# Values of a chunk in one row on TensorE: both halves of the heads behind both masks, in a kernel of linear attention and two expert layers

## The chip, the cores and the metric

One core of one Trainium2 chip. The metric is device time in microseconds (us), as a median of runs. "PE" is TensorE's matmuls, "PEld" its weight loads, DVE is VectorE, ACT is ScalarE, POOL is GpSimd, SP is SyncE, which here issues most DMAs.

## What is computed

The reference has three parts, one behind the other. The first is a linear attention with a complex decay for every channel, 4 batches of 8 heads, 768 steps, 48 channels per head:

```
for t in range(768):
    S = a[t] * S + outer(k[t], v[t])      # a complex, normalised to |a| <= 0.999
    y[t] = q[t] @ real(S)                 # per batch and head, S is 48 x 48
x = y as (3072 tokens, 384)
h = x @ w_in                              # 384 -> 2048
x = (h * tanh(softplus(h))) @ w_out       # 2048 -> 384
e = argmax(x @ w_gate + modality_bias)    # 8 experts, the best one per token
out = gate * relu(x @ w1[e]) @ w2[e]      # 384 -> 1024 -> 384
```

## The kernel before, in words

**Tiling.** The attention is cut into 24 chunks of 128 steps (six per batch, all eight heads at once), and two chunks form a unit. There are 12 units. A unit of 256 tokens then goes through the first dense layer in eight steps (`moe1_h`, `moe1_act`, `moe1_o`): on TensorE a half of such a step is nine matmuls into `ph` or six into `po`, about a microsecond of work. Such a half, or a few small matmuls, is what stands between the pieces of the attention on TensorE. The expert layer follows from about 655 us on.

**A chunk of attention.** `att_scores` (lines 541 to 584) makes for each group of four heads (`hg` 0 and 1):
- scores: four products of keys and queries into the PSUM tile `ps`, of which there is one buffer (lines 550 to 555);
- mask: one VectorE multiplication of `ps` with the causal mask into the SBUF tile `sc` (lines 557 to 559);
- values: for each head `v` times `sc`, and for all but the first chunk of a batch the old state `s0` times the queries added to it, into the PSUM tile `py` (lines 561 to 568). Even heads write partitions 0 to 63 of `py`, odd heads 64 to 127, so each of these matmuls uses 64 of TensorE's 128 columns. In the trace every product of this float32 kind is two matmuls.

At the end ScalarE copies `py` to `Y` (line 580), and two DMAs of SP's queue write it to `xT`, from which the dense layer reads. `sc` of both groups and `Y` share one tag with two buffers (`tag="sc"`, `bufs=2` of the pool `apw`), so the three tiles of a chunk go round in two places: the mask of group 1 of a chunk takes the place that `Y` of the chunk before had.

In these texts S0 and S1 are the scores of the two groups, M0 and M1 their masks, V0 and V1 their values.

**What sets the order.** Nothing is issued directly. Each piece of work is a "strand" of operations with a due time, and `Plan.run` (lines 165 to 247) simulates the engines by a table of costs (`Queue.cost`, lines 264 to 282) and writes out one fixed order for each engine. An operation is ready when the one before it in its strand has its planned result. `part()` (lines 118 to 123) turns several operations of one engine into a single one, between which nothing else is put. The table charges 0.11 us for a product whose output has 64 partitions, and nothing for going from one kind of matmul to another.

`state` of the next chunk (`att_state`) and its `scores` wait for the mark `y` of the chunk, which stands behind V1. `s0`, which V0 and V1 read, is the state that the strand of the chunk before has made (the wait for `s`, lines 573 and 574).

The lines of the profile are all L261 (the place in `Queue` where every operation is issued), so the groups are told apart by the names of their tiles.

Of the kernel before, what the change touches and what calls it, by code (L numbers as in the profile page):

```python
# [540 lines left out]
def att_scores(g, ins, ci, xT):  # L541
    nc, p = g.nc, g.plan
    u, c = divmod(ci, 2)
    cc = ci % 6
    QK, v, s0 = g.QK[u], g.vt[ci % 2], g.st[ci % 2]
    p.wait(f"QK{u}_0")
    py = g.aps.tile([128, 4, 128], F32, tag="py", name=f"py{ci}")
    sc = {}

    def scores(hg):  # L550
        ps = g.aps.tile([128, 4, 128], F32, tag="ps", name=f"ps{ci}_{hg}")
        with p.part():
            for h in range(4):
                nc.tensor.matmul(ps[:, h, :], QK[hg][0:96, h, 1, c, 0:128], QK[hg][0:96, h, 0, c, 0:128], start=True, stop=True)
        return ps

    def mask(hg, ps):
        sc[hg] = g.apw.tile([128, 4, 128], F32, tag="sc", name=f"sc{ci}_{hg}")
        nc.vector.tensor_mul(sc[hg], ps, g.mask.to_broadcast([128, 4, 128]))

    def values(hg):
        with p.part():
            for h in range(4):
                hh = hg * 4 + h
                o = py[(hh % 2) * 64:(hh % 2) * 64 + 64, hh // 2, :]
                nc.tensor.matmul(o, v[:, hh, :], sc[hg][:, h, :], start=True, stop=cc == 0)
                if cc > 0:
                    nc.tensor.matmul(o, s0[:, hh, :], QK[hg][0:96, h, 0, c, 0:128], start=False, stop=True)

    mask(0, scores(0))  # L570
    p.wait(f"QK{u}_1", f"v{ci}")
    ps = scores(1)
    if cc > 0:
        p.wait(f"s{ci - 1}")
    values(0)
    mask(1, ps)
    values(1)
    p.mark(f"y{ci}")
    Y = g.apw.tile([128, 4, 128], F32, tag="sc", name=f"Y{ci}")
    nc.scalar.copy(out=Y, in_=py)  # L580
    dst = xT.rearrange("(p a e) t -> a e p t", a=2, e=48)
    for a in range(2):
        with p.behind(f"x{u}"):
            nc.sync.dma_start(out=dst[a, :, :, ci * 128:(ci + 1) * 128], in_=Y[a * 64:a * 64 + 48])


def attention(g, ins, units, xT):
    p = g.plan
    for u in units:
        with p.strand(f"lanes {u}", {0: 5, 1: 45, 2: 100}.get(u, due(u) - 75)):  # L590
            if u:
                p.wait(f"D{u - 1}")
            if u > 2:
                p.wait(f"h{u - 3}")
            att_lanes(g, ins, u)
        with p.strand(f"ends {u}", {0: 8, 1: 55, 2: 110}.get(u, due(u) - 62)):
            p.wait(f"D{u}")
            att_ends(g, u)
        att_repack(g, u)
        if u + 1 < NU:  # L600
            att_load(g, ins, u + 1)
        for c in range(2):
            ci = 2 * u + c
            with p.strand(f"load v {ci}", due(u) - 50 if u else -17.5):
                if ci > 1:
                    p.wait(f"y{ci - 2}", f"s{ci - 2}")
                with p.behind(f"v{ci}"):
                    g.nc.sync.dma_start(out=g.vt[ci % 2][:, :, 0:48], in_=ins["v"][ci])
            with p.strand(f"state {ci}", due(u) - 45 + 6 * c):
                if ci:  # L610
                    p.wait(f"s{ci - 1}")
                att_state(g, ins, ci)
            with p.strand(f"scores {ci}", due(u) - 43 + 6 * c):
                if ci:
                    p.wait(f"y{ci - 1}")
                att_scores(g, ins, ci, xT)
# [1191 lines left out]
```

## Time and profile before

| | |
|---|---|
| median of 3 runs | 955.14 us (952.89 to 955.41) |
| the profiled execution, its own time | 951.5 us |
| its span in the profile | 949.6 us |
| PE busy | 874.9 us (92%), 6401 matmuls |
| PEld busy | 828.8 us (87%) |
| DVE busy | 732.7 us (77%) |
| ACT busy | 668.8 us (70%) |
| POOL busy | 175.2 us (18%) |
| mean granted clock of TensorE | 0.974 of full speed |

A busy share is a mean over stages with different limits: until about 70 us, when the attention has its first scores, TensorE is mostly idle, and the attention's last values are at 621 us. Matmuls overlap each other, and the end of one is modelled, so what a piece costs TensorE is best read from start to start: from its first row in the timeline to the first row of the piece behind it.

### The profile page before, as it was taken

To read this page: it belongs to the slowest core of one execution; us is meant where nothing else is said; L and a number is where in the kernel's file an instruction comes from. 1 tells how busy PE (TensorE), PEld (TensorE's weight loads), DVE (VectorE), ACT (ScalarE), POOL (GpSimd) and SP (SyncE) were. 2 spreads that over 40 slices of the span, in tenths; PEclk is the share of its full clock that TensorE was granted. 3 is DMA by queue.
4 is the path that set the end of the run, shared out by engine and by line. 5 is a ranking of instruction groups with operands and counts; after the bars stand their busy time and mean duration, and the time that the engine had idled before them with its cause. 6 is when DMAs were issued, how large, how long until landed. Compare 5 with 4: busy or idle time off the path is not lost.

```text
span 949.6 us, 17369 instructions
## 1 busy us (share of the span) xinstructions
PE 874.9 (92%) x6401; PEld 828.8 (87%) x6401; DVE 732.7 (77%) x1517; ACT 668.8 (70%) x1093; POOL 175.2 (18%) x237
## 2 busy tenths in 40 slices
PE   1489899999999999998999999999899999999993
PEld 1267789999999989998999999999799999999883
DVE  4989788889898988798889899764699865565541
ACT  5786969787968787887788787767754556556551
POOL 1021202112120221030303020202112034332211
PEclk9979899999999999999999999999799999999997
DMA  9923323425252534233524142305654767666730
GB/s 306 347 68 89 96 71 113 112 78 124 78 124 67 135 93 109 68 95 107 134 68 123 46 102 67 93 26 194 225 190 136 247 216 237 218 223 212 235 123 7
DMA packets 102749, 128.22 MB, mean 135 GB/s; under 512 B 34601, under 2 KB 76599, under 8 KB 102656
## 3 DMA queue, kind: packets, MB, share of 16 engines
q1 hardware_dynamic: 89680, 89.00, 31.4%
q0 software_dynamic: 12976, 38.03, 13.3%
q8 instruction: 52, 0.85, 0.4%
q14 instruction: 41, 0.34, 0.1%
HBM read 93.74 MB, written 14.82 MB: 114 GB/s over the span
## 4 chain that ended last, share of the span: by engine, by line
PE 46%; ACT 22%; issue 11%; DMA 9%; DVE 8%; POOL 2%; SPq 0%; ACTq 0%; POOLq 0%; DVEq 0%
PE ph L261 11%; PE po L261 10%; ACT u L261 9%; PE py L261 5%; PE ps L261 5%; DMA out<-oss,tt 5%; PE qhs L261 4%; ACT X L261 3%; ACT S L261 3%; PE pst L261 3%; PE qos L261 3%; PE pl L261 2%; DVE ar L261 1%; ACT gh L261 1%; ACT v L261 1%
## 5 line engine op out<-in xcount | busy, mean ns | idle before, releaser
L261 ACT ACTIVATE u<-u 128x512 f32<-128x512 f32 x384 | 237.8, 629 | 6.5
L261 PE MATMUL po<-wt,gh 128*128 128x392 f32 x768 | 206.7, 350 | 2.3 <-ACT gh L261 2.0
L261 PE MATMUL ph<-xh,wt 128*128 128x256 f32 x1152 | 193.5, 288 | 6.6 <-ACT xh L261 4.1
L261 PEld LDWEIGHTS ph<-xh,wt 128*128 128x128 f32 x1152 | 163.5, 191 | 11.5 <-ACT xh L261 4.8
L261 PEld LDWEIGHTS po<-wt,gh 128*128 128x128 f32 x768 | 135.2, 190 | 6.6 <-issue 2.9
L261 PE MATMUL po<-wt,gl 128*128 128x392 f32 x384 | 132.0, 344 | 2.1 <-DVE gl L261 2.1
L261 PE MATMUL qos<-v,hhs 128*128 128x384 f32 x432 | 111.8, 339 | 0.0
L261 POOL DMA_DIRECT2D QK<-X x120 | 65.6, 554 | 230.7 <-ACT xs L261 72.1
L261 PE MATMUL qhs<-y,v 128*128 128x256 f32 x792 | 103.1, 283 | 0.0
L261 PE MATMUL ph<-xl,wt 128*128 128x256 f32 x576 | 101.5, 285 | 1.6 <-DVE xl L261 1.4
L261 PEld LDWEIGHTS qhs<-y,v 128*128 128x128 f32 x792 | 98.7, 189 | 0.0
L261 DVE TENSOR_TENSOR v<-r1s,v 128x1536 fp32r<-128x1536 f32 x30 | 52.7, 1757 | 49.0 <-ACT v L261 46.1
L261 ACT ACTIVATE u<-ph 128x512 f32<-128x512 f32 x96 | 56.7, 591 | 45.6 <-PE ph L261 41.9
L261 DVE SCALAR_TENSOR_TENSOR u<-u,ph 128x512 f32<-128x512 f32 x96 | 65.5, 683 | 26.3 <-ACT u L261 26.1
L261 PEld LDWEIGHTS ph<-xl,wt 128*128 128x128 f32 x576 | 82.7, 191 | 3.2 <-DVE xl L261 3.1
L261 DVE TENSOR_TENSOR gl<-u,gh 128x512 fp32r<-128x512 f32 x96 | 65.7, 686 | 14.6 <-ACT gh L261 14.5
L261 ACT ACTIVATE gh<-u 128x512 fp32r<-128x512 f32 x96 | 60.1, 627 | 23.7 <-DVE u L261 23.6
L261 PEld LDWEIGHTS po<-wt,gl 128*128 128x128 f32 x384 | 72.9, 190 | 3.5 <-DVE gl L261 3.3
L261 PEld LDWEIGHTS qos<-v,hhs 128*128 128x128 f32 x432 | 75.3, 188 | 0.1
L261 POOL DMA_INDIRECT xg<-x,tt x27 | 42.3, 1568 | 167.5 <-PE pt L261 116.6
L261 PE MATMUL qos<-v,hls 128*128 128x384 f32 x216 | 72.6, 336 | 0.0
L261 ACT ACTIVATE hhs<-qhs 128x512 fp32r<-128x512 f32 x48 | 28.7, 599 | 59.2 <-PE qhs L261 58.2
(149 smaller groups left out, 1598.3 us busy)
## 6 DMA issues: line engine op xcount, KB each, us to landing
r0s<-in_w SPq DMA_DIRECT2D x30, 768.0 KB, 4.5
r1s<-in_w SPq DMA_DIRECT2D x30, 768.0 KB, 4.8
QK<-X POOLq DMA_DIRECT2D x72, 96.8 KB, 3.4
QK<-X SPq DMA_DIRECT2D x72, 96.8 KB, 3.7
r<-in_wo SPq DMA_DIRECT2D x8, 768.0 KB, 7.9
r<-in_wi SPq DMA_DIRECT2D x8, 768.0 KB, 13.5
X<-in_q POOLq DMA_DIRECT2D x12, 384.0 KB, 4.9
A<-in_ai POOLq DMA_DIRECT2D x12, 384.0 KB, 4.5
```

Source lines behind the costliest of these rows:

```text
L261: self.plan.add(self.name, *cost[:2], lambda: real(*a, **k), *cost[2:])
```

## The change

S1 no longer has V0 right behind it: M1 is planned straight after S1, and V0 and V1 together become one operation of the plan, which waits for both masks (and for the old state). No instruction is added or taken away, and no tile changes.

```
     def values(hg):
-        with p.part():
-            for h in range(4):
-                hh = hg * 4 + h
-                o = py[(hh % 2) * 64:(hh % 2) * 64 + 64, hh // 2, :]
-                nc.tensor.matmul(o, v[:, hh, :], sc[hg][:, h, :], start=True, stop=cc == 0)
-                if cc > 0:
-                    nc.tensor.matmul(o, s0[:, hh, :], QK[hg][0:96, h, 0, c, 0:128], start=False, stop=True)
+        for h in range(4):
+            hh = hg * 4 + h
+            o = py[(hh % 2) * 64:(hh % 2) * 64 + 64, hh // 2, :]
+            nc.tensor.matmul(o, v[:, hh, :], sc[hg][:, h, :], start=True, stop=cc == 0)
+            if cc > 0:
+                nc.tensor.matmul(o, s0[:, hh, :], QK[hg][0:96, h, 0, c, 0:128], start=False, stop=True)
 
     mask(0, scores(0))
     p.wait(f"QK{u}_1", f"v{ci}")
-    ps = scores(1)
+    mask(1, scores(1))
     if cc > 0:
         p.wait(f"s{ci - 1}")
-    values(0)
-    mask(1, ps)
-    values(1)
+    with p.part():
+        values(0)
+        values(1)
     p.mark(f"y{ci}")
```

## Rows read from the trace of the kernel before

**Rows 1.** Busy time by stretch: stretch and length, PE, PEld, DVE, ACT, POOL, clock, DMA.

```profile
150.00:250.00 100.00, 99.08 (x770) 95.23 (x770) 87.77 (x189) 82.39 (x144) 16.48 (x28) 1.00 0.36 99
250.00:350.00 100.00, 96.58 (x764) 92.56 (x763) 88.67 (x188) 81.13 (x145) 16.50 (x28) 1.00 0.36 96
...
625.00:700.00 75.00, 69.81 (x466) 67.74 (x466) 46.47 (x93) 53.94 (x82) 10.41 (x6) 0.93 0.49 167
```

**Rows 2.** Waits of PE and PEld: who for whom, us in total, times, longest.

```profile
PE ph L261 <- ACT xh L261: 4.1, 2, 2.7
PE pst L261 <- ACT KT L261: 2.7, 4, 0.8
...
PEld py L261 <- issue: 0.9, 4, 0.3
```

**Rows 3.** Instructions of the tile py: count, shortest, median and longest in ns.

```profile
L261 ACT COPY Y<-py x24: 567/587/598, 74.0 to 621.4; 128x512 f32<-128x512 f32 x24
```

**Rows 4.** Timeline of PE, one chunk: start, length of the run of rows, what.

```profile
269.01 1.05 PE L261 MATMUL ps<-QK 96*128 96x128 f32 x8
269.82 0.60 PE L261 MATMUL po<-wt,gh 128*128 128x392 f32 x2
...
270.97 0.51 PE L261 MATMUL ph<-xh,wt 128*128 128x256 f32 x3
...
272.04 1.05 PE L261 MATMUL ps<-QK 96*128 96x128 f32 x8
273.02 0.45 PE L261 MATMUL py<-sc,vt 128*64 128x128 f32 x4
273.29 0.40 PE L261 MATMUL py<-QK,st 96*64 96x128 f32 x4
273.51 0.44 PE L261 MATMUL py<-sc,vt 128*64 128x128 f32 x4
273.73 0.44 PE L261 MATMUL py<-QK,st 96*64 96x128 f32 x4
274.10 0.63 PE L261 MATMUL ph<-xh,wt 128*128 128x256 f32 x3
...
275.37 0.45 PE L261 MATMUL py<-sc,vt 128*64 128x128 f32 x4
```

**Rows 5.** Timeline of PE, first chunk of a batch (no old state).

```profile
224.65 1.06 PE L261 MATMUL ps<-QK 96*128 96x128 f32 x8
225.63 0.66 PE L261 MATMUL py<-sc,vt 128*64 128x128 f32 x8
226.22 0.55 PE L261 MATMUL pkt<-ident,X 128*128 128x128 f32 x3
```

**Rows 6.** Timeline of PE, a chunk whose S1 is followed by other work.

```profile
569.09 1.48 PE L261 MATMUL pst<-vt,KT 128*96 128x48 f32 x16
570.50 0.45 PE L261 MATMUL py<-sc,vt 128*64 128x128 f32 x4
```

**Rows 7.** Timeline of PE from 96 us, where weights are still being prepared.

```profile
96.46 0.94 PE L261 MATMUL pl<-r,ident 128*128 128x384 f32 x2 [1.79 <-ACT wt L261]
```

**Rows 8.** Timeline of DVE: an M0, the M1 of rows 4, and a later M1.

```profile
183.20 0.69 DVE L261 TENSOR_TENSOR sc<-ps,mask 128x512 f32<-128x512 f32 x1 [0.53 <-PE ps L261]
...
273.81 0.68 DVE L261 TENSOR_TENSOR sc<-ps,mask 128x512 f32<-128x512 f32 x1
...
430.88 0.69 DVE L261 TENSOR_TENSOR sc<-ps,mask 128x512 f32<-128x512 f32 x1 [0.31 <-DMA xT<-Y]
```

**Rows 9.** Timeline of PE: the S1 behind the first mask of rows 8, and that ahead of the last.

```profile
184.07 1.06 PE L261 MATMUL ps<-QK 96*128 96x128 f32 x8
...
428.34 1.12 PE L261 MATMUL ps<-QK 96*128 96x128 f32 x8
```

**Rows 10.** Instructions of the tile Y: its DMAs, from issue to landing.

```profile
DMA to landing us min/median/max: 1.9/2.6/4.7
```

**Rows 11.** Timeline of PE at the end of the first dense layer.

```profile
673.62 0.45 PE L261 MATMUL po<-wt,gl 128*128 128x392 f32 x1 [1.25 <-DVE gl L261]
```

## The prediction, made before the run

> **What bounds the kernel now.** I read the busy time by stretch first: between 150 and 350 us TensorE's matmuls cover 97 to 99% of the time, at a granted clock of 1.00 (2.4 GHz), with VectorE at 88% and ScalarE at 82% [rows 1]. The second view, the waits of TensorE, says what the rest is: a few gaps, such as those ahead of `pst` and `ph`, 2.7 and 4.1 us in all. Ahead of the values there is next to nothing, 0.9 us of issue in four pieces; TensorE never waits there for a mask [rows 2]. So from about 107 to 657 us TensorE sets the pace, and what shortens its sequence should shorten the kernel. The third view, TensorE's timeline around one chunk, tells what that sequence costs, read from start to start [rows 4].
>
> S0, with dense-layer matmuls behind it, takes 269.82 - 269.01 = 0.81 us. S1, of the same eight matmuls but with values behind it, takes 273.02 - 272.04 = 0.98. A values piece takes 274.10 - 273.02 = 1.08: its four blocks start 0.27, 0.22 and 0.22 us apart, and from the fourth to the next kind of work it is 0.37. A dense half inside a dense stretch takes 272.04 - 270.97 = 1.07, behind scores 270.97 - 269.82 = 1.15, and between V0 and V1 275.37 - 274.10 = 1.27. So entering the 64-column kind costs about 0.10 to 0.17 us plus 0.05 in its first block, and leaving it about 0.15 plus 0.10 in what follows. These costs are paid twice per chunk today. There are 24 chunks [rows 3], and in the timeline each has other work between V0 and V1; 22 have V0 right behind S1.
>
> **The change, part by part.** It removes no instruction and no DMA, and moves none past SP's or POOL's queue; M1 moves forward in VectorE's order, V0 backward in TensorE's.
>
> *One entry and one exit fewer.* Before, from S1 to the end of V1: 0.98 + 1.08 + 1.27 + 1.08 = 4.41 us. After, S1 is followed by the dense half: 0.81; that half stands behind scores and ahead of values: 1.07 + 0.08 + 0.10 = 1.25; the joined values are eight blocks: 0.27 + 6 x 0.22 + 0.37 = 1.96. Sum 4.02, a saving of 0.39 us. In the four first chunks of a batch a values piece is eight matmuls, 226.22 - 225.63 = 0.59 us, and S1 takes 0.98 there too [rows 5]: I take 0.17 for S1, 0.10 to 0.15 for the joined piece, 0.30 in all. In the two chunks where `pst` stands between S1 and V0 it takes 1.41 us [rows 6]; there S1's 0.17 is not paid, and the saving is 0.20 for the values and 0.10 for the entry, 0.30. Sum: 18 x 0.39 + 4 x 0.30 + 2 x 0.30 = 8.8 us.
>
> What of it lies on the path: the first two chunks run before 82 us, and at 96 us TensorE waits 1.79 us for ScalarE's work on weights [rows 7], which the change doesn't speed up. I count their 0.7 us as lost: 8.1. Bounds from rows: none of the switching cost comes back (0) if it is only put elsewhere, and at most 24 x 0.44 = 10.6 if V0's first block also loses its 0.05.
>
> The Trainium skill, "TensorEngine Tiling (Array Packing)", section Key Properties, says that changing the tiling mode drains TensorE. "TensorE: Matmul & The Clock Gate", section Single matmul latency, puts the drain of a matmul at some 0.17 us. An estimate from these two pages is 2 x 0.17 = 0.34 us per chunk, 7.5 for the 22 chunks that count. The rows give 8.1 for these, and I keep the rows.
>
> *The new wait: V0 behind M1.* Now M1 has all of V0 and the half behind it, 2.35 us, to finish. After, it has the one half (1.25 us) that the plan puts there, or two. In rows 4 S1's last matmul ends at 272.04 + 1.05 = 273.09. If M1 followed at once it would end 0.68 later [rows 8], at 273.8, while the half ends at 272.04 + 0.81 + 1.25 = 274.10: no stall, 0.3 us to spare. The nearest case in the trace is S1 itself, which must wait until M0 has freed `ps`: M0 ends at 183.89 [rows 8] and S1 starts at 184.07 [rows 9], with one half between S0 and S1 and no idle time. Behind a waiting values row stands all of TensorE's work, and behind `y` the copy `Y`, the DMAs to `xT` and the next state; they all come earlier or later together with V1's end, which by the sum comes 0.39 us earlier. I cost the wait itself at nothing; its ends are a gain of 0 and a loss of 1.1 us per chunk (the second rival).
>
> *M1 and the place of Y.* M1 of the second chunk of a unit writes where `Y` of the first stood. Once M1 already waited for that DMA, 0.31 us [rows 8]; the DMAs land after 1.9 to 4.7 us [rows 10]. There S1 ends at 428.34 + 1.12 = 429.46, M1 can't start before 430.88, and with one half between, TensorE would come to V0 at about 430.4 and wait until 431.6. I take one such stall of 1.1 us; bounds 0 and 12 of them, 13 us.
>
> **Sum.** 8.1 - 1.1 = 7.0 us. The profiled execution took 951.5 us, so one like it would take 944.5; the median stands 3.6 us above it, and 955.1 - 7.0 = 948.1 us is the forecast. Behind 657 us everything is taken to shift as a whole, since route, gathers and weight loads are started by work that comes after the attention.
>
> **Rivals.** *Part is given back.* The plan is one long simulation, and M1's new place shifts every later choice. Gaps such as those ahead of `pst` (2.7 us) and `ph` (4.1 us) [rows 2] could double; and at the end of the dense layer TensorE waits for VectorE's and ScalarE's work, 1.25 us before one matmul [rows 11], so part of the gain may be lost to waits there. For: TensorE is at 69.8 of 75 us in that stretch [rows 1]. Against: these gaps hang on copies that don't move. Price: 2 to 5 us off the gain, 950 to 953 us.
>
> *TensorE waits for M1.* The table of costs knows neither the place of `Y` nor how late VectorE really is. If the plan leaves one half between S1 and V0 and M1 comes as late as now, then in rows 4 it ends at 274.49, 0.4 after the 274.10 at which the half ends, and the stall eats the saving. In the chunk at 428 us M1 ends at 431.57 against 430.4: 1.1 lost. Halfway, 0.75 - 0.39 = 0.36 us lost in each of 22 chunks: 8 us slower, 963. It decides from the point where M1 starts more than 0.7 us behind S1's last matmul. For: VectorE is 88% busy, and M1 today starts 0.72 and 1.42 us behind it in these two chunks. Against: today's M1 is planned behind V0, so some 0.9 us of that is the plan's own choice, and the plan puts values in only when their masks are due; it can put in a second half.
>
> "TensorE: Matmul & The Clock Gate" of the Trainium skill, section The mechanism (Part 3), says that matmuls start and end strictly in program order and only weight loads are pulled ahead. By it the dense work behind a waiting V0 could not step in, as this rival has it; TensorE's idle time ahead of `pst` in the trace agrees [rows 2].
>
> *The change does not join what it says*: the plan might still put work between the values. Against: a `part()` is one operation, so I give it nothing.
>
> **How the numbers follow.** Main case 0.70: 943.5 to 951.5, the predicted time 948.1. Given back 0.18: 950 to 953. Waits for M1 0.12: about 963. About 0.3% (2.9 us, so 952.2 us) is what a measurement of this kernel can tell from no change. The main case lies wholly below that, and 0.10 of the second: faster 0.80. The rest of the second, 0.08, is the same; the third is slower, 0.12. The range goes from 943.5 (no stall for `Y`, no loss ahead of 107 us, and the 0.05) to 953, which leaves out the third case and the edges.
>
> **What would show it.** Right: one run of `py` rows of 32 matmuls per chunk (16 in four of them) of about 1.96 us, S1 at 0.81, M1 directly behind S1 on VectorE, no new wait of `py` for `sc`, and the attention's last values about 7 to 8 us earlier than 621. Wrong: `py` waiting for VectorE's `sc`, by more than 0.39 us per chunk; values still at 0.22 us per block but a first and last block that grew; or last values earlier by 8 us with the end of the kernel where it was.

## The result and the profile after

| | before | after |
|---|---|---|
| median of the runs made side by side | 954.62 us (952.89 to 955.41, 4 runs) | 943.51 us (941.0 to 945.95, 4 runs) |
| ratio, 95% interval | | 0.9886 [0.9855, 0.9917] |
| the profiled execution, its own time | 951.5 us | 941.0 us |
| mean granted clock of TensorE | 0.974 | 0.979 |

The kernel is faster by 11.1 us; by the interval of the ratio, by 7.9 to 13.8 us. The direction was forecast. The size was not: 7.0 us were forecast, and the new median lies at the very edge of the range.

The profile's first part after the change, span and busy time of each engine:

```profile
span 939.2 us, 17356 instructions
PE 862.4 (92%) x6401; PEld 824.3 (88%) x6401; DVE 732.4 (78%) x1517; ACT 667.8 (71%) x1093; POOL 173.3 (18%) x237
```

There are as many matmuls as before, and TensorE is busy 12.5 us less. VectorE and ScalarE do the same work in the same time. So the gain is in what the matmuls cost where they stand, and, as is shown below, in a few us of TensorE's clock.

Busy time by stretch after the change, the stretches of [rows 1]:

```profile
150.00:250.00 100.00, 98.06 (x775) 94.99 (x775) 87.26 (x185) 82.88 (x148) 16.45 (x28) 1.00 0.35 96
250.00:350.00 100.00, 95.79 (x766) 92.63 (x766) 87.49 (x188) 80.75 (x143) 16.47 (x28) 1.00 0.36 96
```

From 150 to 250 us there are 775 matmuls in place of 770, in less busy time. From 250 to 350 us there are 766 for 764, and 4.2 us without a matmul in place of 3.4: a part of what they saved is now spent waiting.

TensorE's timeline after the change, the chunk of [rows 4], from its S1 to the end of its values (lines left out are marked with dots):

```profile
267.49 1.05 PE L261 MATMUL ps<-QK 96*128 96x128 f32 x8
268.30 0.59 PE L261 MATMUL ph<-xh,wt 128*128 128x256 f32 x3
...
269.44 0.49 PE L261 MATMUL pkt<-ident,X 128*128 128x128 f32 x3
269.87 0.45 PE L261 MATMUL py<-sc,vt 128*64 128x128 f32 x4
...
271.46 0.44 PE L261 MATMUL py<-QK,st 96*64 96x128 f32 x4
271.83 0.55 PE L261 MATMUL pkt<-ident,X 128*128 128x128 f32 x3
```

S1 takes 268.30 - 267.49 = 0.81 us, as forecast, and the eight blocks of values stand in one row of 271.83 - 269.87 = 1.96 us, as forecast. The joined rows of the chunks from 122 us on, first chunks of a batch aside, all have this length but one. That one is the tenth chunk, at 278.69 us, where the place of `Y` matters. Timeline of VectorE there, its M1:

```profile
280.42 0.69 DVE L261 TENSOR_TENSOR sc<-ps,mask 128x512 f32<-128x512 f32 x1 [3.22 <-DMA xT<-Y]
```

and of TensorE, S1 and the values of the same chunk:

```profile
275.50 1.12 PE L261 MATMUL ps<-QK 96*128 96x128 f32 x8
...
278.69 0.45 PE L261 MATMUL py<-sc,vt 128*64 128x128 f32 x4
...
279.40 0.44 PE L261 MATMUL py<-QK,st 96*64 96x128 f32 x4
281.17 0.45 PE L261 MATMUL py<-sc,vt 128*64 128x128 f32 x4 [1.32 <-DVE sc L261]
```

Two things are to be seen. VectorE sat idle 3.22 us until the DMA of the earlier `Y` had left its place, and TensorE waited 1.32 us for the mask. And the wait stands in the middle of the row: V0 ran at 278.69, 1.7 us before its chunk's M1 began, and only V1 waited. The plan treats the joined values as one operation that waits for both masks; on the chip V0 waits for M0 alone.

The tile `Y` after the change, who waited for it (us, times), and its DMAs:

```profile
  DVE sc L261: 10.2, 8
...
DMA to landing us min/median/max: 1.9/2.7/6.6
```

So M1 now waits for the place eight times, 10.2 us in all, where before one 0.31 us was found [rows 8]. Seven of the eight end before TensorE comes to V1.

The waits of TensorE after the change (who for whom, us in total, times, longest):

```profile
PE ph L261 <- DVE xl L261: 5.3, 11, 1.3
...
PE pkt L261 <- ACT KT L261: 3.8, 8, 0.6
PE ph L261 <- ACT xh L261: 2.4, 5, 0.6
```

and two of these kinds in the kernel before:

```profile
PE pkt L261 <- ACT KT L261: 2.1, 4, 0.6
...
PE ph L261 <- DVE xl L261: 1.4, 5, 0.5
```

So the wait of `ph` for `xh` is smaller than in [rows 2], and small waits for `xl` and `KT` have grown.

**Where the time went, by stretch.** I took anchors that stand in both traces and compared their starts, and between them summed every piece of TensorE from its first row to the first row of the next piece, idle time apart.

- Before the first S0: 66.29 us before, 64.24 after, 2.05 us. No engine's order differs up to there. The clock does, as the next fence shows.
- First S0 to the first `ph` of the second unit (four chunks): 88.32 to 86.13, 2.2 us. A part of it is the clock, see below.
- From there to the first product of the expert layer (20 chunks): 528.54 to 522.55, 6.0 us. Pieces without waits (`pkt` holds the turned keys, `pst` what the next state is made of): values -3.54, scores -2.93, `po` -0.99, `pst` -0.52, `pkt` and `ph` together +0.48, `pr` -0.15, in all -7.6, of which some 1.7 are the clock, see below. Waits: `py` +1.32, `pkt` +1.74, `ph` +0.73, `pst` -1.65, `po` -0.57, in all +1.6.
- The expert layer: 251.8 against 252.0 us. It moves as a whole.

Busy time by stretch ahead of the attention, the kernel before:

```profile
50.00:60.00 10.00, 7.59 (x35) 4.95 (x34) 9.90 (x13) 9.97 (x18) 5.36 (x10) 0.67 0.35 93
60.00:70.00 10.00, 10.00 (x50) 8.27 (x50) 6.90 (x9) 7.96 (x14) 0.10 (x1) 0.65 0.29 68
```

and the kernel after:

```profile
50.00:60.00 10.00, 7.54 (x44) 5.27 (x43) 9.73 (x12) 9.97 (x18) 5.46 (x10) 0.83 0.39 100
60.00:70.00 10.00, 10.00 (x57) 7.57 (x58) 9.11 (x13) 7.93 (x15) 0.00 (x0) 0.83 0.22 61
```

The column behind POOL is the granted clock: 0.65 to 0.67 in one profiled execution, 0.83 in the other, in a stretch in which both do the same. The kernels of the experiments fall on both sides (0.67 and 0.72 for the first below, 0.80 and 0.83 for the second, whose order is the same up to there). So these 2 us belong to the execution and not to the change. Without them the pair of profiles differs by 10.4 - 2.05 = 8.4 us.

The clock differs in two later places too. After TensorE's waits at 96 us [rows 7] it is 0.50 (1.2 GHz) for a while, before:

```profile
97.64:104.46 6.82, 4.65 (x16) 3.63 (x17) 6.02 (x10) 6.82 (x12) 0.00 (x0) 0.50 0.01 2
```

and after:

```profile
101.24:104.65 3.41, 3.41 (x18) 3.39 (x18) 3.30 (x5) 3.41 (x8) 0.00 (x0) 0.50 0.00 0
```

Three matmuls into `ph` take 1.01 us at the low clock where they take 0.51 at the high one (rows below and [rows 4]), so half of the busy time there is lost, 2.3 against 1.7 us. The first S0 of the kernel before, still in the slow stretch, costs 0.3 us more than the other's. By this estimate 0.9 of the 2.2 us ahead of the second unit are the clock. The other place is the longest wait for `xh` in the kernel before, TensorE's timeline:

```profile
442.26 0.92 PE L261 MATMUL ph<-xh,wt 128*128 128x256 f32 x3 [2.75 <-ACT xh L261]
443.39 1.01 PE L261 MATMUL ph<-xl,wt 128*128 128x256 f32 x3 [0.22 <-DVE xl L261]
...
445.98 0.87 PE L261 MATMUL ph<-xh,wt 128*128 128x256 f32 x6
...
448.12 0.52 PE L261 MATMUL ph<-xh,wt 128*128 128x256 f32 x3
```

and the windows of the same stretch:

```profile
442.30:445.80 3.50, 3.28 (x14) 2.99 (x15) 2.48 (x4) 3.47 (x5) 0.00 (x0) 0.51 0.22 90
```

Up to 445.98 fifteen matmuls take 3.50 us, the wait of 0.22 taken off; the next eighteen take 2.14, so fifteen would take 1.8. That is a loss of some 1.7 us. The changed kernel has no wait of this length there and none of the loss: its clock is 1.00 from 150 to 650 us.

### The profile page after: what moved, and what is told of

The parts are those of the page before. It is cut to its first block, busy times and chain, and to the rows that moved or that the text cites. A ratio compares the mean times of both kernels' runs of the same rounds, so it can differ in the third digit from the quotient of the medians.

```text
span 939.2 us, 17356 instructions
## 1 busy us (share of the span) xinstructions
PE 862.4 (92%) x6401; PEld 824.3 (88%) x6401; DVE 732.4 (78%) x1517; ACT 667.8 (71%) x1093; POOL 173.3 (18%) x237
## 4 chain that ended last, share of the span: by engine, by line
PE 33%; ACT 26%; DVE 14%; issue 12%; DMA 10%; POOL 2%; SPq 0%; ACTq 0%; POOLq 0%; DVEq 0%
ACT u L261 11%; PE ph L261 8%; PE po L261 7%; DMA out<-oss,tt 5%; ACT S L261 4%; PE qhs L261 4%; ACT X L261 3%; DMA xT<-Y 3%; PE qos L261 3%; PE ps L261 3%; PE py L261 3%; DVE S L261 3%; ACT gh L261 2%; DVE ar L261 2%; PE pst L261 2%
## 5 line engine op out<-in xcount | busy, mean ns | idle before, releaser
L261 PEld LDWEIGHTS ph<-xh,wt 128*128 128x128 f32 x1152 | 162.6, 190 | 10.4 <-ACT xh L261 4.7
L261 DVE TENSOR_TENSOR gl<-u,gh 128x512 fp32r<-128x512 f32 x96 | 65.7, 685 | 11.4 <-ACT gh L261 11.1
```

What stands on the lines that cost most here:

```text
L261: self.plan.add(self.name, *cost[:2], lambda: real(*a, **k), *cost[2:])
```

## Experiments

All times are medians, with the kernel before run beside them on the same chip (953.3 to 953.9 us); a ratio is taken within the rounds in which both ran, so it is not quite the quotient of the medians.

**1 and 2. One more change of kind per chunk.** Both kernels add the same unread float32 product of 128 columns to the joined row, once between V0 and V1, once behind V1. The plan charges both alike, so the order of everything else is the same in the two; what differs is one exit from the 64-column kind and one entry.

```diff
     with p.part():
         values(0)
+        nc.tensor.matmul(px[:, 0, :], QK[1][0:96, 0, 1, c, 0:128], QK[1][0:96, 0, 0, c, 0:128], start=True, stop=True)
         values(1)
```

> The changed kernel with one more full-width float32 product (128 columns, a repeat of the first score of group 1 into the free place of ps) in every chunk, between V0 and V1 of the joined row; nothing reads it. Theory A (switching): the row is cut again, so each chunk pays one more exit and one more entry. The profile should show V0 at about 1.08 us from start to start up to the extra product, and the whole row (V0, product, V1) at 1.08 + 0.15 to 0.20 + 1.08 = 2.3 to 2.4 us where the changed kernel has 1.96. Time about 24 x 0.4 = 9 us over the changed kernel: 951 to 954 us. Rival B (order): the gain comes from M1's earlier place and the waits that went with it, and switching costs little: the row is 1.96 + 0.20, the time 943.5 + 24 x 0.2 = 948 us.

```diff
     with p.part():
         values(0)
         values(1)
+        nc.tensor.matmul(px[:, 0, :], QK[1][0:96, 0, 1, c, 0:128], QK[1][0:96, 0, 0, c, 0:128], start=True, stop=True)
```

> The same extra product, behind V1 at the end of the joined row instead of between V0 and V1: the plan is charged the same, the order of everything else is the same. Theory A: the product costs itself and no further exit and entry of the 64-column kind, about 0.2 us per chunk, so 943.5 + 5 = 948 us, and 5 to 7 us below the kernel that has it between V0 and V1. Rival B: both kernels take the same time, within 2 us.

Measured: between, 972.23 us (ratio 1.0183 [1.0138, 1.0229]); behind, 963.05 (1.0094 [1.0066, 1.0123]). TensorE's timeline with the product between:

```profile
289.36 0.45 PE L261 MATMUL py<-sc,vt 128*64 128x128 f32 x4
...
290.44 0.49 PE L261 MATMUL px<-QK 96*128 96x128 f32 x2
290.86 0.45 PE L261 MATMUL py<-sc,vt 128*64 128x128 f32 x4
291.12 0.40 PE L261 MATMUL py<-QK,st 96*64 96x128 f32 x4
291.35 0.44 PE L261 MATMUL py<-sc,vt 128*64 128x128 f32 x4
...
291.94 0.55 PE L261 MATMUL pkt<-ident,X 128*128 128x128 f32 x3
```

and with it behind:

```profile
325.88 0.45 PE L261 MATMUL py<-sc,vt 128*64 128x128 f32 x4
...
327.84 0.49 PE L261 MATMUL px<-QK 96*128 96x128 f32 x2
328.09 0.49 PE L261 MATMUL ph<-xh,wt 128*128 128x256 f32 x2
```

Between, V0 takes 1.08 us, the product 0.42 and V1 1.08 again (its blocks start 0.26 and 0.23 us apart, as V0's), 2.58 together. Behind, the row takes 1.96 and the product 0.25, 2.21. The same matmuls cost 0.37 us more when the kind changes twice more. These two rows are not of the same chunk. Set chunk against chunk, with the nine matmuls behind the row, the difference is 0.30 us in the four first chunks of a batch and 0.35 to 0.40 in the others (one chunk at 79 us, in which TensorE waited, left out). At 0.37 us, 24 chunks give 8.9 us; the medians stand 9.2 us apart, the two ratios 0.0089 of 954, 8.5 us. That one more exit and entry costs some 0.3 to 0.4 us is shown. A change of the output tile alone is not what costs: a dense half into `ph` behind one into `po` takes 1.07 us [rows 4], no more than its nine matmuls in a row.

The level of both was missed. The product behind should cost 24 x 0.25 = 6 us (0.24 to 0.25 us where dense work follows, 0.32 or 0.33 where `pkt` or `pl` does) over the changed kernel's 943.5; 13 us more came. The waits of TensorE say where, with the product behind:

```profile
PE ph L261 <- ACT xh L261: 13.0, 4, 7.5
```

With the product between it is 12.7 us, three times. The product's charge in the table gave another order, and in this order the dense layer's input `xh` comes late. The next kernels are about this.

**3 and 4. The change in one chunk of each unit.** One joins the values only in the second chunk of a unit, the other only in the first.

The first, the second having `c == 0`:

```diff
-    mask(1, scores(1))
-    if cc > 0:
-        p.wait(f"s{ci - 1}")
-    with p.part():
-        values(0)
-        values(1)
+    if c == 1:
+        mask(1, scores(1))
...
+        with p.part():
+            values(0)
+            values(1)
+    else:
+        ps = scores(1)
...
+        with p.part():
+            values(0)
+        mask(1, ps)
+        with p.part():
+            values(1)
```

> The change in the second chunk of each unit alone (12 of 24 chunks); the first chunk of a unit keeps the order of before. Theory A: the saving goes by the number of joined rows, about half of the 11 us: 948 to 950 us. In the profile the joined chunks have one run of 32 values in 1.96 us and the others two of 1.08. Rival B (a lucky order): no such proportion, the time is near that of either kernel, 943.5 or 954.6.

> The change in the first chunk of each unit alone (the other half of the chunks than in the kernel that took 973 us). Theory A with a plan's luck of its own on top: TensorE's values and scores give half of their 8 us, and the rest of the time is what this plan's waits for xh make of it; 945 to 952 us if those waits stay near the 4 us of the kernel before, above 960 if they grow past 15 us again. Rival S (mixing two orders in a unit is what costs): 965 to 975 us, with waits for xh above 15 us.

Measured: second chunk only, 973.48 us (1.0218 [1.0149, 1.0286]); first chunk only, 966.61 (1.012 [1.0072, 1.0168]). The first of these was a plain miss, and the second came out where the rival put it. Yet the saving is there: over the same 20 chunks the values take 1.85 us less than before and the scores 1.35 less with the second chunk joined, 1.84 and 1.38 with the first: half of 3.54 and 2.93 each time. It is lost elsewhere. Waits of TensorE with the second chunk joined:

```profile
PE ph L261 <- ACT xh L261: 17.6, 5, 7.1
```

TensorE's timeline at the longest of them:

```profile
602.84 1.01 PE L261 MATMUL ph<-xh,wt 128*128 128x256 f32 x3 [7.06 <-ACT xh L261]
```

and the whole kernel's timeline ahead of it:

```profile
595.61 0.57 ACT L261 COPY Y<-py 128x512 f32<-128x512 f32 x1
596.20 0.79 SPq L261 DMA_DIRECT2D xT<-Y  x2
...
598.65 0.38 SPq L261 DMA_DIRECT2D xr<-xT  x1
601.94 0.84 ACT L261 ACTIVATE xh<-xr 128x768 fp32r<-128x768 f32 x1 [5.66 <-DMA xr<-xT]
```

Read from below: TensorE has nothing to do until `xh` is there, `xh` needs `xr`, `xr` the `xT` that this unit's last `Y` was written to. From the copy of `Y` to `xh` it is 601.94 + 0.84 - 595.61 = 7.2 us. The attention of the unit has ended too late for the dense layer behind it: its first S0 comes 32 us after the first `ph` of the unit before, against 21.9 us in the kernel before and 21.8 in the changed one. The first matmuls behind the gap take 1.01 us where such a run elsewhere takes about 0.51 [rows 4], twice as long: the granted clock from 598.4 to 608.6 us is 0.50 (1.2 GHz), and TensorE had stood still for 7.06 us in it. In the windows of this kernel that shows as a clock below 1:

```profile
450.00:550.00 100.00, 91.33 (x694) 87.80 (x694) 80.46 (x176) 71.66 (x128) 15.34 (x26) 0.95 0.32 88
550.00:650.00 100.00, 91.26 (x717) 87.96 (x716) 77.72 (x208) 70.84 (x125) 12.57 (x22) 0.95 0.24 64
...
598.40:608.60 10.20, 4.83 (x21) 4.53 (x22) 9.72 (x25) 2.63 (x4) 0.00 (x0) 0.50 0.12 39
```

The changed kernel does 778 and 782 matmuls in the first two of these stretches, at a clock of 1.00 in both.

The rival of these two kernels, that mixing two orders in a unit is slow by itself, is not needed: the kernels of experiments 1, 2, 7, 10 and 11 mix nothing, and TensorE waits 10.6 to 13.0 us for `xh` in them too. What the mixing may add is not separated.

**5. The change without the first two chunks.** They run ahead of 82 us, and their saving had been counted as lost.

Set against the kernel of experiment 3:

```diff
-    if c == 1:
+    if ci >= 2:
```

> The change from the third chunk on; the first two chunks (those ahead of 82 us) keep the order of before. The prediction took their saving for lost, while in the profiles the changed kernel is 2.0 us ahead at its first score already and 4.2 us ahead at the start of the second unit's dense work. If the prediction's term holds, this kernel takes the changed kernel's time, 943 to 945 us. If the first two chunks' new order gives the 4 us, it takes about 947.5 us, and the second unit's dense work starts at about 154 us as before.

Measured: 946.81 us (943.95 to 954.48, 10 runs; 0.9941 [0.991, 0.9972]), 3.3 us above the changed kernel, with intervals that overlap. In the trace the first S0 starts at 64.37 and the second unit's first `ph` at 151.52 us, 87.15 apart, against 86.13 with the whole change, 1.0 us. But the clock differs between the two here as well. The windows of this kernel:

```profile
94.84:101.67 6.83, 5.14 (x18) 3.46 (x16) 6.03 (x9) 6.83 (x13) 0.00 (x0) 0.50 0.01 3
```

Half of the busy time at 0.50 is 2.6 us, against 1.7 in the changed kernel: 0.9 of the 1.0 us is the clock, by this estimate. So the two traces don't show that the first two chunks' saving reaches the end. Against the kernel before, whose order on TensorE is the same up to there, the S0 of the third chunk already comes 0.4 us earlier behind the first S0; the two chunks at 122 and 132 us give the other 0.7 us of 88.32 - 87.15. The remaining 2.3 us between this trace and the changed kernel's come after 150 us, where TensorE waits 7.3 us for `xh` in place of 2.4.

**6 to 8. Another plan.** If the orders of kernels 3 and 4 suffer because the table takes a DMA for landed after 1.8 us, where [rows 10] have a median of 2.6, a lag of 2.8 us should mend it. The third of these kernels is the one before under the same table, so that the change can be compared under a second plan.

```diff
         if "dma" in what:
             run = out.shape[-1] * 4
-            return 0.65, 1.8, n * out.shape[0] * 4e-6 / (0.32 if run > 1000 else 0.25)
+            return 0.65, 2.8, n * out.shape[0] * 4e-6 / (0.32 if run > 1000 else 0.25)
```

Joined in the second chunk only:

> The kernel that joins the values in the second chunk of each unit alone, written out by a plan whose cost table charges a DMA 2.8 us behind its issue instead of 1.8. The one without that took 973 us: in its profile ScalarE stands at xh for the DMA xr<-xT 12.3 us in four pieces, which it never does in the kernels before and after, and TensorE waits 17.6 us for xh. Theory O (order): joining in one chunk of two costs nothing, the plan had put xh and what stands behind it on ScalarE ahead of the time at which the DMAs land. With the longer DMA these waits fall below 4 us each and the time comes to about half the gain, 947 to 952 us. Rival S: mixing the two orders in a unit is slow by itself; it stays near 970 us.

The changed kernel:

> The changed kernel under the plan with the longer DMA (2.8 us). Theory O: the changed kernel has no wait of xh for its DMA and only 2.4 us of TensorE for xh, so there is little to win: 940 to 946 us, values rows as before at 1.96 us. If it moves by more than 5 us either way, the plan's order is worth as much as the change itself.

The kernel before:

> The kernel before under the plan with the longer DMA (2.8 us), so that before and after can be compared under a second plan. Theory A (switching): TensorE's values, scores and what follows them cost what they did, 8 us more than in the changed kernel under the same plan; 950 to 957 us. Rival B (a lucky order): the two kernels under this plan take the same time, within 3 us.

Measured: second chunk only 978.05 us (1.026 [1.0188, 1.0331]); changed 958.29 (952.35 to 963.62, 10 runs; 1.0046 [1.0005, 1.0087]); before 967.73 (963.94 to 968.37; 1.0136 [1.0062, 1.0209]). The two whole kernels are slower than with 1.8 us, and the first can't be told from its 973.48. ScalarE's waits ahead of `xh` for the DMA, 12.3 us in experiment 3, are gone with the longer lag, yet TensorE waits 21.3 us for `xh`. That theory falls. But the change itself is worth 967.73 - 958.29 = 9.4 us under this plan too (by the ratios 1.0136 - 1.0046 = 0.009, 8.6 us; the two intervals overlap a little, the runs themselves don't), and the wait for `xh` is about equal on the two sides. The changed kernel's waits here:

```profile
PE ph L261 <- ACT xh L261: 10.7, 5, 4.2
```

and those of the kernel before:

```profile
PE ph L261 <- ACT xh L261: 9.1, 4, 5.3
```

The switching is there: over 20 chunks the values take 3.53 us less than in the kernel before under this plan and the scores 3.51 less. The rest of the difference was not taken apart; the two profiled executions are 4.1 us apart ahead of these chunks and 3.0 behind them, with other clocks, so that 9.4 is a rough figure for the change.

**9. Attention due earlier.** The kernel of experiment 3 with all due times of the attention 8 us earlier.

```diff
-            with p.strand(f"scores {ci}", due(u) - 43 + 6 * c):
+            with p.strand(f"scores {ci}", due(u) - 51 + 6 * c):
```

(and the same for its loads, scans and states and for the copies of its result, `xh` and `xl`).

> The kernel with the change in the second chunk alone (973 us), all due times of the attention 8 us earlier. Theory: TensorE's 17.6 us for xh come because the attention's preparation on VectorE and ScalarE falls behind the dense work in the order; ranked earlier it should keep ahead: waits for xh below 8 us and 950 to 960 us. Rival: the order hardly moves by ranks, since operations go by when they are ready; the time stays within 5 us of 973.

Measured: 972.91 us (1.0204 [1.0156, 1.0253]) against 973.48. TensorE still waits 13.2 us for `xh`. Due times 8 us earlier change nothing in the time.

**10 and 11. The saving told to the plan, and `xl` last.** The first charges 0.1225 us for a product of the 64-column kind, 1.96 / 16 from the joined row, in place of 0.11. The second adds to it that the dense half uses the low part `xl` of its input last, as the next kernel does.

```diff
-            if what == "transpose" or out.shape[0] == 64:
+            if out.shape[0] == 64:
+                return 0.1225, 0.2
+            if what == "transpose":
                 return 0.11, 0.2
```

> The changed kernel under a plan that charges 0.1225 us (1.96 us for 16) for a product of values instead of 0.11, so that a joined row has in the plan the length that it has in the trace. If the plan's order gains by true costs: 938 to 942 us. If each new order is a draw of its own, the time lies anywhere from 940 to 960 us, with values, scores and what follows them costing TensorE the same as in the changed kernel, and the difference in its waits for xh.

> The plan with the longer values and x's low part last in a dense half, together. If both are worth what the waits say: about 3 us below the kernel with the longer values alone, from TensorE's waits for xl (5.3 us in the changed kernel) falling below 1 us.

Measured: 962.52 us (1.0101 [1.0052, 1.015]) and 958.16 (952.72 to 963.35, 10 runs; 1.005 [1.0021, 1.0078]). The first was a miss, above both its forecasts. A table nearer to the chip gave a worse order: the saving is there (values -3.54, scores -2.67), and the wait for `xh` is 10.6 us in both. The second lies some 4 us below the first, as forecast, though their runs overlap.

**12. `xl` last in the changed kernel.** Its largest new wait of `ph` is that for `xl`, 5.3 us.

```diff
-            for pt, xv in ((0, xh), (0, xl), (1, xh)):
+            for pt, xv in ((0, xh), (1, xh), (0, xl)):
```

> The changed kernel with the nine matmuls of a dense half in another order: x's high part times both parts of the weights first, x's low part last. In the changed kernel's profile TensorE waits 5.3 us in 11 pieces for VectorE's xl, right behind the first three matmuls of a unit; with six matmuls (0.7 us) ahead of xl those pieces should nearly vanish. If they are on the path, 943.5 - 4 = 939 to 940 us; if the attention's chain holds the units anyway, 943 us and the wait is seen elsewhere, at xh or KT.

Measured: 942.62 us (937.95 to 951.36, 10 runs; 0.9908 [0.9867, 0.995]), which can't be told from the changed kernel's 0.9886 [0.9855, 0.9917]. The wait for `xl` fell to 0.9 us. What was late next is the turned keys; the waits of TensorE:

```profile
PE pkt L261 <- ACT KT L261: 6.7, 8, 1.0
```

That is 2.9 us more than in the changed kernel. From the second unit's first `ph` to the expert layer this execution is 2.6 us shorter, but ahead of the attention its clock was 0.50 to 0.60 and its first S0 came at 68.13 us. No version here is shown to beat the changed kernel.

A further `sc` place of its own for `Y`, which would take the 3.22 us wait away, wasn't tried.

## Why the prediction was right, and where it was off

**One entry and one exit fewer: right, in its size too, chunk by chunk.** Its 4.02 us from S1 to the end of V1 are 0.81 + 1.24 + 1.96 = 4.01 in the four chunks where the plan left one dense half between (V0 starts 2.05 or 2.06 us after S1). The joined row in a first chunk of a batch takes 1.02 us, where 1.18 - 0.10 to 0.15 was taken. For the 20 chunks behind 150 us the sum comes to 8.1 less the 0.78 of the two chunks at 122 and 132 us, 7.3. The pieces measured 7.6, but some 1.7 of that is the clock at 442 us, so 5.9 are left: scores and values give 6.5, `pst` 0.5, and the other pieces cost some 1.1 more, of which the cause is open. Experiments 1 and 2 give 0.30 to 0.40 us per chunk by rows and 0.35 to 0.38 by time, 7 and 8 the gain under a second plan. The estimate from "TensorEngine Tiling (Array Packing)" (Key Properties) and "TensorE: Matmul & The Clock Gate" (Single matmul latency) of the Trainium skill, a drain at each change of kind, had 0.34 us per chunk. The runs agree that a change of kind is paid for, with 0.30 to 0.40 us for one exit and entry.

**The first two chunks: open.** The step "I count their 0.7 us as lost" is not decided. Experiment 5 and the changed kernel differ by 1.0 us up to 150 us, and by the estimate above 0.9 of it is the clock behind the waits at 96 us, in one execution of each. That leaves about nothing for the two chunks, which fits the step; the medians, 3.3 us apart with overlapping intervals, don't settle it.

**V0 behind M1: right that it costs next to nothing, by another reason.** V0 does not wait for M1 at all; V1 does, four blocks later. So M1 has 0.81 + 1.24 us and V0's 0.9 on top. M1 was often later than the 0.7 us behind S1's last matmul that the rival named as its point: between 0.04 and 1.8 us, once 3.8, and in nine chunks it ended after V0 had begun. Only in one did TensorE wait. Also, in most chunks the plan put a second piece between (2.3 to 3.8 us from S1 to V0). The rival "TensorE waits for M1", 963 us, fell: 1.32 us in all.

**M1 and the place of `Y`: right in size, in part by luck.** One stall of 1.1 us was taken, and one of 1.32 came. But M1 waits for the place in eight chunks of the twelve that the upper bound held, not in one, and the stall stands ahead of V1 and not of V0. Had V0 needed M1, as the prediction took it, the wait at 278.69 us alone would have been 280.42 + 0.69 - 278.69 = 2.4 us.

**The sum: near, in part by luck.** For the 20 chunks it had 7.3 - 1.1 = 6.2 us, and the trace has 6.0. But these 6.0 are made of other terms: 5.9 from the pieces and 1.7 from the clock at 442 us, less 1.6 for new waits, of which the sum had 1.1. Neither the gain of the clock nor the waits of `pkt` and `ph` stood in the sum, and they nearly cancel. The four chunks ahead give 1.3 us without the clock, where the sum had 0.78. Together that is 7.3 us for 7.0. The other 3 us between the two profiled executions are the clock up to 105 us. The medians differ by 11.1 us with an interval of 7.9 to 13.8, and by 9.4 under the second plan; how much of the distance from 7.3 to 11.1 is the change and how much the executions' clock, the runs don't tell.

**The range.** Its lower end, 943.5 us, does not follow from the terms named for it: 8.8 + 24 x 0.05 = 10.0 us, or the upper bound of 10.6, off 955.1 is 944.5 to 945.1. The new median of 943.51 is below that, so that it lies in the range is luck. And 0.3% is too narrow for what a run can tell: single runs of the kernel before, beside the experiments, took 947.8 to 959.4 us.

**The rival "part is given back"** named the right danger and the wrong place and price. In the changed kernel waits took back 1.6 us of 7.6. But many further orders gave back far more: experiments 1 to 4 and 9 to 11 ended at 958 to 973 us with all of the saving in the rows, or their half of it (in experiment 1 that of the scores). Those of 5 and 12 did not, at 946.81 and 942.62. It had been priced at 2 to 5 us; it is some 13 to 25 us where it struck (963.05 less the 949.5 of the changed kernel with its added product in experiment 2, 973.48 less some 949 with half the saving in experiment 3), through `xh`, whose wait went from 4.1 to 2.4 us with the change and to 10.6 to 17.6 us there, and through the lower clock behind each gap. That the change as it stands met a good order could not have been read from the rows; a chance of 0.18 was low for it. Why an order makes the attention of some units late is not settled: the DMA's lag, the due times and the charge for values were each changed, and none mended it.

Last, where the joining comes from: with M1 straight behind S1 and V0 and V1 left as two operations, the plan writes out the same order on every engine as for the change. So by the order alone it is M1's new place that brings the values together, not the one operation.

## What to carry to other kernels

Read what a change between kinds of matmul costs from start to start, at both ends and in the neighbours' first rows, and multiply by the count: here 4.02 us were forecast for a chunk's pieces and 4.01 measured. Where a program writes the order, compare an edit under at least two plans, since a changed order can cost more than the edit saves; the first row to look at is then the wait of the busiest engine for its input from the other stage. A wait that an edit moves ahead of a joined operation binds only the instructions that read its result, so look at which of them come first. And before a difference between two profiles is put down to an edit, set their granted clocks side by side, stretch by stretch: here some 3 of 10.4 us between the two were the clock ahead of 105 us.

## What the runs showed of the hardware

With the same order of work up to the first scores (eleven profiled executions: all but those of experiments 6 to 8), the granted clock of TensorE in ten us of the stretch from 50 to 70 us was anything from 0.50 to 0.83, and the first scores started between 64.2 us (clock 0.83) and 68.1 us (0.50 and 0.60). A pair of profiles can so differ by 2 to 4 us before the edit is reached. Behind a wait of TensorE of 2.75 us the clock was 0.51 for 3.5 us, which cost some 1.7 us on top of the wait.

A float32 product of two matmuls of 128 columns takes 0.24 to 0.25 us behind the values where dense work follows (0.32 or 0.33 where `pkt` or `pl` does) and 0.42 us between them; the row that follows then pays again for its first block (0.26 in place of 0.22 us).
